# Attention, routed experts and a second layer on one core: first-expert weights loaded later and rounded on GpSimd, v crossed one step later, sums work moved out of the first expert, all rests on VectorE

## The chip, the cores and the metric

The kernel runs on one core of a Trainium2 chip. The metric is device time in microseconds (us), lower is better. In the tables PE is TensorE (PEld its weight loads), DVE is VectorE, ACT is ScalarE, POOL is GpSimd and SP is the engine that here only issues transfers. An engine takes its instructions in the order in which they stand in its queue, so an instruction that waits holds all behind it.

## The reference, cut to what matters

```python
# q, k, v: (8, 8, 576, 64); tokens N = 4608, model width 512
scores = scale * np.matmul(q_c, k_c.transpose(0, 1, 2, 4, 3))   # chunks of 64 tokens
attn = softmax(scores); x = np.matmul(attn, v_c)                # -> x: (4608, 512)
do_compute = x @ w_skip > 0
e_idx = np.argmax(x[do_compute] @ w_gate, axis=1)               # 8 experts, one per token
for e in range(8):
    h = np.maximum(xc[mask] @ w1[e], 0.0)                       # 512 -> 1024
    y[mask] = gate_w[mask, None] * (h @ w2[e])                  # 1024 -> 512
x[do_compute] = xc + y
h = np.maximum(np.maximum(x @ w1, x @ w2), x @ w3)              # 512 -> 768, all tokens
return h @ w_out
```

## The kernel before, in words

**Attention and routing.** The 4608 tokens are 36 tiles of 128. A loop of 36 steps does one tile per step, and each stage of a tile runs one step behind the stage before it. In step t TensorE multiplies the exponentials of tile t-2 with v (`xp`), makes the scores of tile t (`sc`), turns exponentials (`trp`), q and k of the next pair of tiles (`trq`, `trk`), makes gate logits of tile t-3 (`lp`) and turns x of tile t-2 (`trx`). ScalarE empties the turned tiles (`aT`, `qT`, `kT`, `xt`, `lg`) and takes the exponentials (`ex`). VectorE does row maxima, scaling and routing. GpSimd rearranges q and k (`qr`, `kr`), scatters token numbers (`ids_dram`) and stores x in groups of four tiles (`x_dram`). Half of each v tile must also lie on the other 64 partitions: `cross` copies one half on GpSimd and `cross_up` the other on ScalarE (`vm`); v has eight buffers, and the load of v of tile t+6 is asked for in step t. SP issues the loads of q, k, v and of weights in one queue; the q and k of the last two pairs of tiles come as 16 small transfers each.

**Weights.** Matmuls run in three passes on a rounded part and its rest: `whi` is the weight rounded to fp32r, `wlo` is the raw weight minus `whi`. An expert has eight pieces of 128x1024. Those of the first expert (`raw_e_0` to `raw_e_7`) are loaded and split amid the attention loop: load at step c-5, `whi` on ScalarE at step c, `wlo` a step later on VectorE (two of them on GpSimd), for c in `CUTS` (12, 16, 18, 20, 24, 26, 28, 32). `raw` tiles have three buffers.

**Behind the loop.** Tokens are routed in groups of four tiles, the last four in two groups of two. The first two tiles of expert 0 use tokens known early; its third tile waits for the last groups (`ids_0`, found by a matmul). In the tail TensorE's order is written by hand, and the products of expert 0 (`h`) are placed by `behind` between pieces of routing; the order on the other engines is left to the scheduler after step 33. Then come the third and fourth tile of expert 0, and experts 1 to 7 in the same way, each with the split of the next expert's weights beside it (pieces 1, 3 and 7 take their rests on GpSimd). `sums_ahead` prepares weights of the second layer in chunks: `STEPS` says how many ride with each expert (2, 2, 2, 2, 2, 1, 0, 0).

**The second layer** runs over all tokens from about 500 us on; the change does not touch it.

Of the kernel before, what the change touches and what calls it, by code (L numbers as in the profile page):

```python
# [40 lines left out]
def kernel(  # L41
# [102 lines left out]
    SIZES = [GT] * (NT // GT - 1) + [2, 2]  # L144
# [165 lines left out]
    def scaled(t):  # L310
        xp = units[t // 2]["xp", t % 2]
        g, j = PLACE[t]
        if j == 0:
            if g == len(SIZES) - 1:
                parts = [four_kb([P, 1, XW], F32, f"xg{g}_{i}", True) for i in range(SIZES[g])]
            else:
                parts = [bpool.tile([P, GT, XW], F32, tag="xg", name=f"xg{g}")[:, :SIZES[g], :]]
# [117 lines left out]
    def place(g):  # L435
# [20 lines left out]
        if START[g] >= DIRECT:  # L456
            place_first(g, oh, lo, hi)

    def place_first(g, oh, lo, hi):
        t0, nt = START[g], SIZES[g]  # L460
        found = ps_sm(f"ids_0_ps{g}")[:, :1]
        lo_f = apool.tile([P, 2], F32, tag="lo_f", name=f"lo_f{g}", bufs=1)
        nc.vector.tensor_copy(lo_f, lo[:, :nt])
        hi_f = apool.tile([P, 2], F32, tag="hi_f", name=f"hi_f{g}", bufs=1)
        nc.vector.tensor_copy(hi_f, hi[:, :nt])
        tok = apool.tile([P, 2], F32, tag="tok0", name=f"tok0_{g}", bufs=1)
        nc.vector.tensor_tensor(tok, oh[:, :nt, 0], tok_f[:, t0:t0 + nt], op=ALU.mult)
        for j in range(nt):
            row = apool.tile([P, P], F32, tag="row", name=f"row{t0 + j}")
            nc.vector.tensor_scalar(row, col_f, lo_f[:, j:j + 1], None, op0=ALU.is_equal)  # L470
            val = apool.tile([P, 1], F32, tag="val", name=f"val{t0 + j}")
            link["val"] = nc.vector.tensor_scalar(
                val, col_f[:, 2:3], hi_f[:, j:j + 1], tok[:, j:j + 1], op0=ALU.is_equal, op1=ALU.mult)
            link["found", g] = nc.tensor.matmul(found, row, val, start=j == 0, stop=j == nt - 1)
        nc.vector.tensor_tensor(ids_0[:, 2:], ids_0[:, 2:], found, op=ALU.add)
# [138 lines left out]

    for u in range(5):
# [11 lines left out]
    LAG, late, raws_0 = GT + 5, range(NT - 2), {}  # L627
    HAND = NT - 2
    CUTS = [12, 16, 18, 20, 24, 26, 28, 32]
    ASIDE = (18, 26)  # L630
    routing = {}
    fetch = None
    in_order = ExitStack()
    in_order.enter_context(tc.manual_schedule(engines={mybir.EngineType.PE}))
    by_hand = ExitStack()
    by_hand.enter_context(tc.manual_schedule(
        engines={getattr(mybir.EngineType, n) for n in ("DVE", "Activation", "Pool")}))

    def last_of(t):
        if 0 <= t < NT:  # L640
            g, j = PLACE[t]
            if j + 1 == SIZES[g]:
                return g
        return None

    for t in range(NT + LAG):
        u, s = divmod(t, 2)
        hand = t < HAND
        if t == HAND:
            by_hand.close()  # L650
        ranked = last_of(t - 5) if hand else None
        if ranked is not None:
            rank_out(ranked)
        if hand and t - LAG in late:
# [12 lines left out]
        if 0 <= t - 2 < NT:  # L667
            values(t - 2)
            scaled(t - 2)
        if t >= 2 and t - 2 + NV < NT:  # L670
            load_v(t - 2 + NV)
        if t + 5 in CUTS:
            i = CUTS.index(t + 5)
            with tc.issue_after(link["load"].ins):
                raws_0[i] = load_raw(*expert_src(0, i))
        if t < NT:
            scores(t)
            shift(t)
        if 0 <= t - 1 < NT:
# [3 lines left out]
        if 0 <= t - 3 < NT:  # L683
# [4 lines left out]
        if t < NT:  # L688
            exponentials(t)
        g = last_of(t - 3)  # L690
        if g is not None and hand:
            route(g)
        if 0 <= t - 2 < NT:
            x_transpose(t - 2)
            x_out(t - 2)
        if t < NT:
            cross_up(t)
        if g is not None and not hand:
            route(g)
            gates(g)  # L700
        g = last_of(t - 4)
        if g is not None:
            if t <= HAND:
                gates(g)
            rank_of(g)
            if not t + 1 < HAND:
                rank_out(g)
        g = ranked if hand else last_of(t - 4)
        if g is not None:
# [3 lines left out]
            if g == FIRST or START[g] + SIZES[g] == DIRECT:  # L713
                for i in range(max(late[0], t - LAG + hand), START[g + 1]):
                    send_id(i)
                late = range(START[g + 1], NT - 2)
            if START[g] + SIZES[g] == DIRECT:
                load_ids(ids_0[:, 2:], ids_rows[:, 2:3])
            if g == FIRST:
# [5 lines left out]
        if t in CUTS:  # L725
            i = CUTS.index(t)
            hi_0 = wpool.tile([P, 1024], F32R, tag="w", name=f"whi_e0_{i}")
            lo_0 = wpool.tile([P, 1024], F32R, tag="w", name=f"wlo_e0_{i}")
            nc.scalar.copy(hi_0, raws_0[i])
            ew[0, i] = hi_0, lo_0  # L730
        if t - 1 in CUTS:
            i = CUTS.index(t - 1)
            hi_0, lo_0 = ew[0, i]
            (nc.gpsimd if t - 1 in ASIDE else nc.vector).tensor_tensor(lo_0, raws_0[i], hi_0.bitcast(F32), op=ALU.subtract)
            ew[0, i] = [w.rearrange("p (a b) -> p a b", a=2) if i > 3 else w for w in ew[0, i]]
# [5 lines left out]
        if not hand and t - LAG in late:  # L741
            send_id(t - LAG)
    in_order.close()
# [12 lines left out]
    first_accs = []  # L756

    def first_acc(name):
        if not first_accs:
            two = two_banks("xp" if turns["half"] else "sc", name)  # L760
            turns["half"] = True
            first_accs.extend([two[:, 0], two[:, 1]])
        return first_accs.pop(0)

    turns["half"] = False
# [22 lines left out]
    def mm3(acc, ahi, alo, bhi, blo, first, last, onto=False):  # L788
        nc.tensor.matmul(acc, ahi, bhi, start=first, stop=False, skip_group_check=onto)  # L789
        nc.tensor.matmul(acc, ahi, blo, start=False, stop=False, skip_group_check=onto)  # L790
        return nc.tensor.matmul(acc, alo, bhi, start=False, stop=last, skip_group_check=onto)  # L791

# [5 lines left out]

    KF_ORDER = [6, 7, 4, 5, 0, 1, 2, 3]

    def second(name, key, hhi, hlo, i, xg, ids, tag=None):
# [3 lines left out]
        for n, kf in enumerate(KF_ORDER):  # L805
            bhi, blo = ew[key[0], 4 + kf // 2]
            with tc.issue_after(link["found", 9].ins) if tag and n > 2 else nullcontext():
                mm3(acc, hhi[:, kf, sl], hlo[:, kf, sl], bhi[:, kf % 2, :], blo[:, kf % 2, :], n == 0, n == 7)
        put_back(key, xg, ids, acc)

    def first_tiles(name, e, xT, xgs, idss, between, side=(), behind=None):
# [5 lines left out]
        for n in range(0, 8, per):  # L817
            f0 = KF_ORDER[n]
            acc = (first_acc if e == 0 else ps_mm)(f"h_{name}_{n}")[:, :per * w].rearrange("p (f t) -> p f t", f=per)
            for j in range(per):  # L820
                f = f0 + j
                with tc.issue_after(behind[n + j].ins) if behind else nullcontext():
                    for c in range(KC):
                        ahi, alo = ew[e, c]
                        link["h"] = mm3(acc[:, j, :], ahi[:, f * P:(f + 1) * P], alo[:, f * P:(f + 1) * P],
                            hi[:, c, :], lo[:, c, :], c == 0, c == KC - 1)
# [5 lines left out]
        for i in range(2):  # L832
            second(f"{name}_{i}", (e, i), hhi, hlo, i, xgs[i], idss[i], "tr" if e == 0 else None)
# [30 lines left out]
    STEPS = [2, 2, 2, 2, 2, 1, 0, 0]  # L864
# [124 lines left out]
    xT[0] = rows_T("0", xgs[0])  # L989
# [3 lines left out]
    for t in range(NT - 2, NT):  # L993
# [17 lines left out]
    for e in range(E):  # L1011
# [23 lines left out]
        if e + 1 < E:  # L1035
            with ExitStack() as pinned:
                if e == 0:
                    for k in ("val", "routed"):
# [5 lines left out]
        behind = [link[k] for k in (  # L1044
            ("x", NT - 1), ("logits", NT - 1), ("rank", 8), ("logits", NT - 1), ("found", 8), ("rank", 9),
            ("found", 9), ("found", 9))] if e == 0 else None
        h_e = first_tiles(
            f"{e}", e, xT[e], xgs[e], [idc(e, 0), idc(e, 1)], ahead, side, behind)
        raws = {i: load_raw(*expert_src(e + 1, i)) for i in LATE} if e + 1 < E else {}
        if e == 0:  # L1050
            turn_ahead()
            with tc.issue_after(link["rows"][0].ins), tc.issue_after(link["rows"][1].ins):
                for chunk in later:
                    chunk()
# [5 lines left out]
        with ExitStack() as pinned:  # L1060
            if e == 0:
                single("0_2", (0, 2), *third, turn_next)
                for ins in link["rows"]:
                    pinned.enter_context(tc.issue_after(ins.ins))
            elif e + 1 < E:
# [168 lines left out]
```

## Time and profile before

| what | value |
|---|---|
| median of 3 runs (lowest, highest) | 1087.12 us (1084.63, 1091.06) |
| the profiled execution | 1093.87 us, of it 1092.1 us from first to last instruction |
| TensorE busy in it | 1015.1 us, 93% |
| VectorE, ScalarE, GpSimd busy | 570.8, 431.2, 359.6 us |
| mean granted TensorE clock | 0.961 |

TensorE is busy nearly all the time, so the question for each stretch is why it stood there and at which clock it ran. The stretches used below are the loop until its first long stall (9.63 to 59.81 us), the loop with stalls (to 155.37), its last steps (to 176.17), the tail until the third tile of expert 0 begins (to 218.40), and the rest of expert 0 (to 269.68).

### The profile page before, as it was taken

To read this page: it belongs to the slowest core of one execution; us is meant where nothing else is said; L and a number is where in the kernel's file an instruction comes from. 1 tells how busy PE (TensorE), PEld (TensorE's weight loads), DVE (VectorE), ACT (ScalarE), POOL (GpSimd) and SP (SyncE) were. 2 spreads that over 40 slices of the span, in tenths; PEclk is the share of its full clock that TensorE was granted. 3 is DMA by queue.
4 is the path that set the end of the run, shared out by engine and by line. 5 is a ranking of instruction groups with operands and counts; after the bars stand their busy time and mean duration, and the time that the engine had idled before them with its cause. 6 is when DMAs were issued, how large, how long until landed. Compare 5 with 4: busy or idle time off the path is not lost.

```text
span 1092.1 us, 19781 instructions
## 1 busy us (share of the span) xinstructions
PE 1015.1 (93%) x7570; PEld 867.2 (79%) x7570; DVE 570.8 (52%) x1100; ACT 431.2 (39%) x771; POOL 359.6 (33%) x381
## 2 busy tenths in 40 slices
PE   8978878979999979997998999999999999999996
PEld 7977768958878868885876788888877888888995
DVE  5766756569737376433688833335144443444241
ACT  5867755335425244322444342223222232223231
POOL 4557555545513263311333140123122140124011
PEclk9989978989999989998999899999999999999998
DMA  9999684467738185428998545663566546666581
GB/s 238 266 293 284 182 198 162 139 222 255 285 111 285 56 300 196 164 83 255 289 325 285 174 158 160 200 186 120 164 183 184 151 136 192 191 201 197 190 254 39
DMA packets 212050, 217.14 MB, mean 199 GB/s; under 512 B 47195, under 2 KB 176235, under 8 KB 211936
## 3 DMA queue, kind: packets, MB, share of 16 engines
q1 hardware_dynamic: 198688, 174.16, 54.1%
q0 software_dynamic: 10656, 33.22, 8.6%
q10 hardware_dynamic: 2592, 8.26, 2.0%
q8 instruction: 70, 1.15, 0.4%
q14 instruction: 44, 0.36, 0.1%
HBM read 175.15 MB, written 41.83 MB: 199 GB/s over the span
## 4 chain that ended last, share of the span: by engine, by line
PE 46%; DMA 5%; issue 1%; DVE 1%; POOL 1%; ACT 0%; SPq 0%; POOLq 0%; DVEq 0%; ACTq 0%
PE f_a L789 6%; PE f_a L791 6%; PE f_a L790 6%; PE o L789 5%; PE o L791 4%; PE o L790 4%; PE f_d L789 3%; PE f_d L790 3%; PE f_d L791 3%; DMA ws<-m_sums 3%; PE f_b L789 1%; PE f_b L791 1%; PE f_b L790 1%; DMA m_sums<-n_q 1%; PE trf L963 1%
## 5 line engine op out<-in xcount | busy, mean ns | idle before, releaser
L94 POOL TENSOR_TENSOR fh<-best,fh 128x512 fp32r<-128x512 f32 (+1 forms) x60 | 75.0, 1255 | 356.6 <-ACT fh L93 271.5
L789 PE MATMUL f_a<-x_t,ws 128*128 128x512 f32 (+1 forms) x270 | 100.4, 373 | 2.7 <-ACT u L1128 2.7
L791 PE MATMUL f_a<-x_t,ws 128*128 128x512 f32 (+1 forms) x270 | 100.1, 371 | 0.0
L790 PE MATMUL f_a<-x_t,ws 128*128 128x512 f32 (+1 forms) x270 | 100.0, 371 | 0.0
L789 PE MATMUL h<-xhi,whi_e 128*128 128x256 f32 x256 | 75.3, 295 | 13.5 <-ACTq L1066 7.2
L790 PE MATMUL o<-wlo_m,fh 128*128 128x512 f32 x216 | 84.6, 391 | 0.0
L93 ACT CAST whi_e<-raw_e 128x1024 fp32r<-128x1024 f32 x56 | 57.7, 1050 | 67.0 <-DMA raw_e<-in_moe_w_dram 35.6
L789 PE MATMUL o<-whi_m,fh 128*128 128x512 f32 x216 | 83.9, 392 | 0.0
L791 PE MATMUL o<-whi_m,fh 128*128 128x512 f32 x216 | 83.3, 393 | 0.0
L789 PE MATMUL y<-whi_e,hhi 128*128 128x512 f32 x184 | 74.1, 404 | 0.6 <-ACT hhi L856 0.6
L790 PE MATMUL h<-xlo,whi_e 128*128 128x256 f32 x256 | 74.6, 292 | 0.1
L791 PE MATMUL h<-xhi,wlo_e 128*128 128x256 f32 x256 | 74.1, 291 | 0.0
L791 PE MATMUL y<-whi_e,hlo 128*128 128x512 f32 x184 | 73.2, 401 | 0.2
L790 PE MATMUL y<-wlo_e,hhi 128*128 128x512 f32 x184 | 72.5, 396 | 0.0
L94 POOL TENSOR_TENSOR wlo_e<-raw_e,whi_e 128x1024 fp32r<-128x1024 f32 x21 | 53.0, 2531 | 57.0 <-ACT whi_e L93 55.7
L93 ACT CAST fh<-best 128x512 fp32r<-128x512 f32 (+1 forms) x60 | 34.6, 579 | 89.8 <-DVE best L1119 60.8
L789 PEld LDWEIGHTS h<-xhi,whi_e 128*128 128x128 f32 x256 | 51.1, 199 | 16.3 <-ACTq L1066 10.2
L789 PEld LDWEIGHTS f_a<-x_t,ws 128*128 128x128 f32 x270 | 51.2, 190 | 12.0 <-ACT u L1128 3.5
L1122 ACT COPY p<-f_a 128x512 f32<-128x512 f32 (+1 forms) x45 | 24.4, 545 | 90.8 <-PE f_a L791 90.6
L791 PEld LDWEIGHTS f_a<-x_t,ws 128*128 128x128 f32 x270 | 51.3, 190 | 8.7
L780 POOL DMA_INDIRECT x_dram<-xg,ids_sb x20 | 20.8, 1041 | 112.9 <-DVEq L1004 46.8
L790 PEld LDWEIGHTS f_a<-x_t,ws 128*128 128x128 f32 x270 | 51.2, 190 | 8.5
(230 smaller groups left out, 2699.5 us busy)
## 6 DMA issues: line engine op xcount, KB each, us to landing
ws<-m_sums SPq DMA_DIRECT2D x135, 512.0 KB
raw_e<-in_moe_w_dram SPq DMA_DIRECT2D x64, 512.0 KB
ws<-m_sums SPq DMA_DIRECT2D x45, 256.0 KB
x<-x_dram SPq DMA_DIRECT2D x36, 256.0 KB
x_dram<-xg POOLq DMA_DIRECT2D x8, 1040.0 KB, 7.7
v_all<-in_v_dram SPq DMA_DIRECT2D x32, 256.0 KB
out_dram<-os SPq DMA_DIRECT2D x32, 256.0 KB
m_sums<-n_raw ACTq DMA_DIRECT2D x18, 448.0 KB
```

The costliest lines, as they stand in the source:

```text
L93: nc.scalar.copy(hi, src),
L94: eng.tensor_tensor(lo, src, hi.bitcast(F32), op=ALU.subtract),
L780: ins = nc.gpsimd.indirect_dma_start(out=x_dram[:, :], out_offset=bass.IndirectOffsetOnAxis(ap=ids, axis=0), in_=xg, in_offset=None, bound ...
L789: nc.tensor.matmul(acc, ahi, bhi, start=first, stop=False, skip_group_check=onto)
L790: nc.tensor.matmul(acc, ahi, blo, start=False, stop=False, skip_group_check=onto)
L791: return nc.tensor.matmul(acc, alo, bhi, start=False, stop=last, skip_group_check=onto)
L963: nc.tensor.transpose(tr[:, i * P:(i + 1) * P], row[:, c * P:(c + 1) * P], ident)
L1122: nc.scalar.copy(p1, acc_a)
```

## The change

First, the loads of the first expert's weights are asked for at steps 15 to 27 (before: 7 to 27), five of the eight into buffers of their own; GpSimd rounds seven of them and ScalarE one; VectorE makes all rests. `ROUND` lists piece, step of the load, engine and step of the rounding, step of the rest. Second, `cross(t - 1)` and `cross_up(t - 1)` run in step t, the second between `kT` and `ex`. Third, the last four tiles are one group, and the tail of the loop is written out by hand for four engines, with the first products of expert 0 in eight parts. Fourth, expert 0 gets no chunk of `sums_ahead` (`STEPS`). Fifth, VectorE makes the rests of all experts' weights.

```diff
-    SIZES = [GT] * (NT // GT - 1) + [2, 2]
+    SIZES = [GT] * (NT // GT)
...
+    def head_part(n):
+        hi, lo = HEAD["xT"]
+        if n % 2 == 0:
+            HEAD["acc", n // 2] = first_acc(f"h_0_{n}").rearrange("p (f t) -> p f t", f=2)
+        f = KF_ORDER[n]
+        for c in range(KC):
+            ahi, alo = ew[0, c]
+            link["h"] = mm3(HEAD["acc", n // 2][:, n % 2, :], ahi[:, f * P:(f + 1) * P], alo[:, f * P:(f + 1) * P],
+                hi[:, c, :], lo[:, c, :], c == 0, c == KC - 1)
...
-    CUTS = [12, 16, 18, 20, 24, 26, 28, 32]
-    ASIDE = (18, 26)
+    ROUND = [
+        (0, 15, "Pool", 19, 21),
+        (1, 18, "Pool", 23, 25),
...
+        (4, 26, "Pool", 35, 37),
+        (5, 27, "Act", 36, 37),
+    ]
...
+    def rounded(t):
+        for i, _, eng, at, _ in ROUND:
+            if at == t:
+                ew[0, i] = [wpool.tile([P, 1024], F32R, tag="w", name=f"w{nm}_e0_{i}") for nm in ("hi", "lo")]
+                (nc.gpsimd.tensor_copy if eng == "Pool" else nc.scalar.copy)(ew[0, i][0], raws_0[i])
...
-        if t < NT:
-            cross(t)
+        if t >= 1:
+            cross(t - 1)
...
-        if t < NT:
-            exponentials(t)
+        if t >= 1:
+            cross_up(t - 1)
+        exponentials(t)
...
-        if t < NT:
-            cross_up(t)
...
-            (nc.gpsimd if t - 1 in ASIDE else nc.vector).tensor_tensor(lo_0, raws_0[i], hi_0.bitcast(F32), op=ALU.subtract)
...
+    head_start(xT[0])
+    head_part(0)
+    x_transpose(NT - 1)
+    x_out(NT - 1)
+    rests(36)
+    head_part(1)
+    logits(NT - 1)
+    logits_out(NT - 1)
+    head_part(2)
+    route(LAST_G)
+    gates(LAST_G)
+    rank_of(LAST_G)
+    rank_out(LAST_G)
+    head_part(3)
...
-    STEPS = [2, 2, 2, 2, 2, 1, 0, 0]
+    STEPS = [0, 2, 2, 2, 2, 2, 1, 0]
...
-                    expert_piece(e + 1, i, free.pop(0), nc.gpsimd if i % 2 else None)
+                    expert_piece(e + 1, i, free.pop(0))
```

Where the instructions stand, at three places. The first is SP's queue. `v_all_130` to `v_all_137` are the eight v buffers in turn, so `v_all_135` is here v of tile 13, and `raw_e_0` is piece 0. Before, from the load of v of tile 12 on:

```order
L216 DMA v_all_134<-in_v_dram 128x8x64
L210 DMA qkt_881<-in_q_dram 128x8x128
L210 DMA qkt_881<-in_k_dram 128x8x128
L216 DMA v_all_135<-in_v_dram 128x8x64
L100 DMA raw_e_0_806<-in_moe_w_dram 128x1024
L216 DMA v_all_136<-in_v_dram 128x8x64
L210 DMA qt_1072<-in_q_dram 128x8x128
L210 DMA kt_1073<-in_k_dram 128x8x128
```

And now, one round of the buffers later, from v of tile 21 on:

```order
L216 DMA v_all_135<-in_v_dram 128x8x64
L701 DMA raw_e_0_230<-in_moe_w_dram 128x1024
L216 DMA v_all_136<-in_v_dram 128x8x64
L216 DMA v_all_137<-in_v_dram 128x8x64
L210 DMA qt_2100<-in_q_dram 128x8x128
L210 DMA kt_2101<-in_k_dram 128x8x128
L216 DMA v_all_130<-in_v_dram 128x8x64
L701 DMA raw_e_1_231<-in_moe_w_dram 128x1024
```

Piece 0 stood right behind v of tile 13 and now stands right behind v of tile 21, behind five more pairs of q and k; ahead of v of tile 28 there stood six pieces (0 to 5), and now three (0 to 2).

The second place is GpSimd's queue at step 19, where before no weight stood; now, from the crossing of tile 18 to that of tile 19:

```order
L223 COPY vm_1993<-v_all_132 64x260
L235 COPY qr_1_1995<-qt_1286 128x512
L235 COPY kr_1_1997<-kt_1287 128x512
L502 DMA x_dram<-xg_1501 128x4x520
L709 CAST whi_e_0_2092<-raw_e_0_230 128x1024
L480 DMA ids_dram<-tok_i,rslot_1790 36864x1
L223 COPY vm_2104<-v_all_133 64x260
```

The rounding of piece 0 stands between the store of x and the crossing of tile 19.

The third place is ScalarE's queue at the third tile of expert 0 (`h_2_1s` and `h_2_0s` are the two halves of its product). Before:

```order
L538 CAST xhi_2_4245<-trm_2_0_4247 128x512
L555 ACTIVATE n_q_4256<-n_raw_4254 128x512
L555 ACTIVATE n_q_4272<-n_raw_4270 128x512
L849 ACTIVATE h_2_1s<-h_2_1_4526 128x512
L596 CAST n_raw_4254<-n_q_4256 128x896
L596 CAST n_raw_4270<-n_q_4272 128x896
L598 DMA m_sums_0_149<-n_raw_4254 128x896
L598 DMA m_sums_0_149<-n_raw_4270 128x896
L849 ACTIVATE h_2_0s<-h_2_0_4541 128x512
```

And now:

```order
L539 CAST xhi_2_4186<-trm_2_0_4188 128x512
L929 ACTIVATE h_2_1s<-h_2_1_4435 128x512
L929 ACTIVATE h_2_0s<-h_2_0_4450 128x512
L539 CAST xhi_4479<-trm_0_4481 128x4x128
L936 CAST hhi_2_4433<-trh_2_1_4465 128x512
L936 CAST hhi_2_4433<-trh_2_0_4472 128x512
```

The instructions of two chunks that stood between the two halves are gone from here.

## Rows read from the trace of the kernel before

**Rows 1.** Stretches: length, busy by engine, granted clock, DMA share, GB/s
```profile
9.63:59.81 50.18, 48.55 (x1088) 45.02 (x1091) 37.89 (x107) 39.69 (x83) 25.94 (x49) 1.00 1.09 261
59.81:155.37 95.56, 74.03 (x1531) 67.78 (x1526) 59.57 (x176) 63.74 (x132) 56.36 (x80) 0.87 0.91 241
155.37:176.17 20.80, 20.05 (x447) 18.57 (x445) 16.09 (x47) 16.35 (x36) 12.16 (x22) 0.94 0.84 214
176.17:218.40 42.23, 39.66 (x334) 36.07 (x325) 22.61 (x101) 13.87 (x27) 21.50 (x22) 0.84 0.37 128
218.40:269.68 51.28, 40.94 (x225) 34.69 (x224) 41.88 (x57) 22.20 (x32) 23.74 (x15) 0.90 0.70 237
```
**Rows 2.** Waits of TensorE, 0 to 260 us: total, times, longest
```profile
PE trx L337 <- ACT aT L292: 20.6, 5, 7.0
PE trh L854 <- ACT h_0s L849: 7.3, 1, 7.3
```
**Rows 3.** Waits of ScalarE and GpSimd, 0 to 200 us
```profile
ACT whi_e L729 <- DMA raw_e<-in_moe_w_dram: 14.3, 4, 5.7
...
ACT vm L229 <- DMA v_all<-in_v_dram: 6.4, 3, 5.3
...
POOL vm L223 <- DMA v_all<-in_v_dram: 24.3, 7, 9.7
```
**Rows 4.** Stretches: q and k whole, then in small transfers
```profile
40.00:106.70 66.70, 56.80 (x1246) 52.63 (x1244) 46.80 (x141) 49.44 (x103) 45.16 (x71) 0.95 1.09 287
106.70:144.60 37.90, 33.22 (x700) 30.67 (x701) 26.46 (x84) 27.68 (x59) 21.17 (x29) 0.86 0.64 188
```
**Rows 5.** Timeline of SP: start, length, what; v of tiles 13, 28
```profile
56.59 1.67 SPq L216 DMA_DIRECT2D v_all<-in_v_dram  x1
58.31 2.60 SPq L100 DMA_DIRECT2D raw_e<-in_moe_w_dram  x1
...
144.58 2.16 SPq L216 DMA_DIRECT2D v_all<-in_v_dram  x2
```
**Rows 6.** Timeline of ScalarE, step 12; in brackets idle before
```profile
66.88 1.04 ACT L729 CAST whi_e<-raw_e 128x1024 fp32r<-128x1024 f32 x1 [5.73 <-DMA raw_e<-in_moe_w_dram]
```
**Rows 7.** Timeline at steps 29 and 30, all engines
```profile
149.65 0.41 ACT L229 COPY vm<-v_all 64x260 f32<-64x260 f32 x1 [5.25 <-DMA v_all<-in_v_dram]
...
149.70 0.39 POOL L223 COPY vm<-v_all 64x260 f32<-64x260 f32 x1 [9.66 <-DMA v_all<-in_v_dram]
...
151.82 1.04 ACT L729 CAST whi_e<-raw_e 128x1024 fp32r<-128x1024 f32 x1 [1.76 <-DMA raw_e<-in_moe_w_dram]
...
154.45 0.37 PE L305 MATMUL xp<-v_all,aT 64*64 64x65 f32 x1
```
**Rows 8.** Stretches behind the loop at half the clock
```profile
181.80:195.50 13.70, 13.63 (x124) 12.67 (x120) 7.60 (x41) 3.77 (x9) 5.90 (x7) 0.50 0.23 79
229.60:239.90 10.30, 5.99 (x18) 4.73 (x19) 6.36 (x14) 4.51 (x7) 1.03 (x1) 0.50 0.88 319
```
**Rows 9.** Timeline at the third tile of expert 0
```profile
222.13 6.23 DVE L554 SCALAR_TENSOR_TENSOR n_q<-n_raw,n_q 128x512 int32<-128x512 int32 x2
...
223.11 4.70 POOL L94 TENSOR_TENSOR wlo_e<-raw_e,whi_e 128x1024 fp32r<-128x1024 f32 x2
...
231.08 1.78 ACT L596 CAST n_raw<-n_q 128x896 fp32r<-128x896 f32 x2 [7.47 <-DVE n_q L593]
...
233.91 1.12 PE L854 MATMUL trh<-ident,h_0s 128*128 128x128 f32 x4 [7.34 <-ACT h_0s L849]
```
**Rows 10.** Groups: busy us, mean ns | idle; the third of the whole span
```profile
L235 POOL COPY qr<-qt 128x512 f32<-128x512 f32 x20 | 12.3, 614 | 13.1 <-DMA qt<-in_q_dram 12.1
...
L734 DVE TENSOR_TENSOR wlo_e<-raw_e,whi_e 128x1024 fp32r<-128x1024 f32 x6 | 7.3, 1220 | 15.3 <-ACT whi_e L729 15.3
...
L94 POOL TENSOR_TENSOR wlo_e<-raw_e,whi_e 128x1024 fp32r<-128x1024 f32 x21 | 53.0, 2531 | 57.0 <-ACT whi_e L93 55.7
```
**Rows 11.** Timeline of TensorE where a later expert begins
```profile
403.22 0.58 PE L789 MATMUL h<-xhi,whi_e 128*128 128x256 f32 x1 [7.16 <-ACTq L1066]
```

More of the change, by code (lines that the diff above doesn't have):

```diff
@@ L313, in scaled @@
         if j == 0:
[L314 to L317, printed above, removed]
+            parts = [bpool.tile([P, GT, XW], F32, tag="xg", name=f"xg{g}")]
             groups[g] = parts, apool.tile([P, GT, E + 1], F32, tag="lg", name=f"lg{g}")
@@ L639, in last_of, with weights_ahead @@
     def last_of(t):
[L640 to L646, printed above, removed]
+        return PLACE[t][0] if 0 <= t < NT and PLACE[t][1] == GT - 1 else None
+    def weights_ahead(t):
+        for i, at, *_ in ROUND:
+            if at == t:
+                src, name, shape = expert_src(0, i)
+                with tc.issue_after(link["load"].ins):
+                    if i in (0, 1, 2, 3, 7):
+                        a = shape[0]
+                        nc.sync.dma_start(raws_0[i].rearrange("p (a b) -> p a b", a=a) if a > 1 else raws_0[i], src)
+                    else:
+                        raws_0[i] = load_raw(src, name, shape)
@@ L647 @@
+    for t in range(NT):
         u, s = divmod(t, 2)
[L648 to L651, printed above, removed]
+        ranked = last_of(t - 5)
         if ranked is not None:
             rank_out(ranked)
-        if hand and t - LAG in late:
+        if t - LAG in late:
             send_id(t - LAG)
@@ L666 @@
             nc.gpsimd.tensor_copy(col_f, col_i)
[L667 removed]
+        if t >= 2:
             values(t - 2)
             scaled(t - 2)
[L670 to L675, printed above, removed]
[L676 to L679 removed]
+            if t - 2 + NV < NT:
+                load_v(t - 2 + NV)
+        weights_ahead(t)
+        scores(t)
+        shift(t)
+        if t >= 1:
             exp_transpose(t - 1)
@@ L724 @@
                 fetch = t + 3
[L725 to L733, printed above, removed]
-            (nc.gpsimd if t - 1 in ASIDE else nc.vector).tensor_tensor(lo_0, raws_0[i], hi_0.bitcast(F32), op=ALU.subtract)
-            ew[0, i] = [w.rearrange("p (a b) -> p a b", a=2) if i > 3 else w for w in ew[0, i]]
+        rounded(t)
+        rests(t)
         if t == fetch:
@@ L740 @@
                 gather(xgs[0][j], at[:, j:j + 1], rows)
-        if not hand and t - LAG in late:
-            send_id(t - LAG)
-    in_order.close()
+    LAST_G = len(SIZES) - 1
+    rank_out(LAST_G - 1)
+    cross(NT - 1)
+    cross_up(NT - 1)
+    for t in range(NT - LAG, DIRECT - 4):
+        send_id(t)
+    values(NT - 2)
+    scaled(NT - 2)
+    logits(NT - 3)
+    logits_out(NT - 3)
+    xT[0] = rows_T("0", xgs[0])
+    exp_transpose(NT - 1)
+    x_transpose(NT - 2)
+    x_out(NT - 2)
+    place(LAST_G - 1)
+    for t in range(DIRECT - 4, DIRECT):
+        send_id(t)
+    load_ids(ids_0[:, 2:], ids_rows[:, 2:3])
+    values(NT - 1)
+    scaled(NT - 1)
+    logits(NT - 2)
+    logits_out(NT - 2)
+    rounded(36)
+    head_start(xT[0])
[12 more added lines that the diff above has]
+    head_part(3)
+    head_relu(0)
+    head_relu(1)
+    place(LAST_G)
+    place_first(LAST_G)
+    head_part(4)
+    head_part(5)
+    found_first(LAST_G)
+    head_rest(0)
+    rests(37)
+    head_rest(1)
+    head_part(6)
+    head_part(7)
+    head_relu(2)
+    head_relu(3)
+    head_rest(2)
+    head_rest(3)
+    by_hand.close()
     cp = ps_sm("cnt_ps")[:, :E]
@@ L992 @@
     gather(xgs[0][2], idc(0, 2))
-    for t in range(NT - 2, NT):
+    for t in range(DIRECT, NT):
         send_id(t)
@@ L1064 @@
                     pinned.enter_context(tc.issue_after(ins.ins))
+                for chunk in later:
+                    chunk()
             elif e + 1 < E:
```

146 lines of the change are left out of this document (80 added, 66 removed).

## The prediction

> **What bounds the kernel now.** I read the stretches first [rows 1]. TensorE is the engine that sets the end: in the quiet part of the loop it is busy 48.55 of 50.18 us, 13 steps at 3.86 us each. The next 17 steps take 95.56 us where 17 x 3.86 would be 65.6, so the stretch loses 30 us. The tail (42.23 us) and the rest of expert 0 (51.28 us) lose too: both run in part at the lower clock, and the second has 10 us without TensorE work. The waits of TensorE name what it stood for [rows 2]: 20.6 us in five waits for ScalarE's `aT`, one of 7.3 us for `h_0s`. But `aT` is only next in ScalarE's queue. ScalarE itself [rows 3] waits 14.3 us for raw weights of expert 0 and 6.4 us for v, and GpSimd 24.3 us for v. So the loop is bound by arrivals, through queues that stand in order. Two states of the transfers follow each other [rows 4]: until 106.7 us the DMA share is 1.09 at 287 GB/s, which is full; then, with q and k in small pieces, 0.64 at 188 GB/s, where SP's issuing one by one is the limit.
>
> **The loop: later weights and later crossing.** The decisive arrival is v of tile 28. SP issues it at 144.58 [rows 5], it lands at 149.65, where both ScalarE and GpSimd stood for it [rows 7], and TensorE multiplies with it at 154.45. SP's order decides when it can leave: six weight pieces stand ahead of it before, three now. A piece is 128 x 1024 x 4 bytes = 0.52 MB, 1.8 us at 287 GB/s, and 2.60 us as SP's issue of piece 0 shows [rows 5]. Three fewer are 5.5 to 7.8 us; I take 6, so v lands at 143.7. Before, 4.8 us passed from landing to the product: the crossing, 1.76 us of waiting for another raw piece, its rounding of 1.04 us, then `aT` [rows 7]. Now ScalarE crosses (0.41), and nothing but that stands between: 0.8 us, so the product starts at 144.5 instead of 154.45. That is 10 us. The last steps, 20.80 us, I leave as they are, since their clock and rate are nearly the full ones. Bounds: 0 if the small transfers, which are the same 32, hold v just as long as before; above, the bytes of the stretch, 95.56 x 241 = 23.0 MB less three pieces, 21.4 MB, at 287 GB/s are 75 us, so 21.
>
> The rounding on GpSimd has no row. Nearest are its copy of 128x512 in 614 ns, which doubled is 1.2 us, and its two-input pass over 128x1024 in 2531 [rows 10]; I take 1.3, and GpSimd has time (56.36 busy of 95.56 [rows 1]). Worse is what the rounding waits for. Piece 0 now leaves after v of tile 21: behind the 56.59 of tile 13 [rows 5] come five pairs of q and k (5 x 1.05 MB), eight tiles of v (8 x 0.26) and two stores of x (2 x 1.06), 9.5 MB or 33 us at 287 GB/s, so at 89.7; with the 8.6 us from 58.31 to 66.88 that it took before [rows 5, 6] it lands at 98.3. GpSimd reaches it at the end of step 19, 59.81 + 7 x 3.86 = 86.8. So there is a new wait of 11 us, behind which stand the scatter, the crossing of tile 19 and the next q and k, and TensorE waits for that crossing at step 21 for some 10 us, until about 101. I cost this at nothing: eight more steps bring step 29 to 132, and v of tile 28 is still on the way until 143.7. That is the cover, 11 us; if v came sooner, this wait would be the price.
>
> **The tail.** TensorE is busy 39.66 of 42.23 us [rows 1], but 13.63 of that ran at 0.50 of the clock, the level of 1.2 GHz [rows 8]; the same work at 2.4 GHz is 6.8 us shorter. All of it is still to be done: 32.8 us. Now parts of the first products stand between each link of the routing chain, and the row maxima of the last tile come ahead of the gates of the group before. I take 34.7, a gain of 7.5. Bounds: 9.4 if no idle time stays; a loss of 3 if the thin start still ends in the low clock and VectorE's four rests (4 x 1.22 us [rows 10]) delay routing by 3 of their 4.9.
>
> **The third tile of expert 0.** VectorE worked on sums for two chunks, ScalarE's rounding of them waited 7.47 us, behind it stood `h_0s`, and TensorE waited 7.34 [rows 9]. TensorE then ran at 0.50, 5.99 us busy [rows 8], which costs 3.0. Both chunks leave expert 0: up to 10.3. I take 9.5, since `h_0s` still follows a product that ends shortly before. Bounds 6 and 10.3.
>
> **Later experts.** 21 rests move from GpSimd (2531 ns) to VectorE (1220) [rows 10]: 26 us more on VectorE, which is free for more than that beside TensorE, and raw buffers come free about 1.3 us sooner each. TensorE stood 7.16 us at one start of an expert behind ScalarE's late rounding [rows 11]. I take 1 gained; bounds a loss of 6 (VectorE late with a rest of the hidden layer at six experts, 1 each) and a gain of 6. Here a rule speaks for more. Beside two of GpSimd's rests (4.70 us) two passes of VectorE took 6.23 [rows 9]. The Trainium skill (SBUF — State Buffer, Who interferes with whom) has it that an instruction of VectorE with two inputs in SBUF and one of GpSimd that reads SBUF block each other whole; by that rule VectorE is freed of these blocks, the 7.16 us go altogether, and the sum below is 34 instead of 28. The trace agrees for that pair, but no row ties the 7.16 to it, so I stay with 1.
>
> **Sum.** 10 + 7.5 + 9.5 + 1 = 28 us off the profiled execution of 1093.87 (span 1092.1 and 1.8 around it): 1065.9. That execution is 6.75 above the median of the runs, 1087.12; against the median it is 1059.
>
> **Rivals.**
> A. The loads set the loop's end and it does not move. For it: SP issues the same 32 small transfers, and 37.90 us of the loop pass at share 0.64 [rows 4]. Against it: pieces leave from ahead of v, and the full part before them is shortened by their bytes. Gain 18, time 1069. The Trainium skill (DMA: Bandwidth & Descriptors, Issuing engines are not separate DMA queues) says that transfers of all engines end on the same 16 engines; by it the moved bytes only return later, which is this rival; the share of 0.64 says that there is room for them, so the trace bears it out little.
> B. The chunks stall as much at experts 5 and 6, where they go: 10.3 back, time 1069. For it: VectorE carries the rests as well there. Against: experts 1 to 4 carry two chunks each and show no wait like rows 9.
> C. The stalls all go, v included: loop gain 21, time 1048. For it: the bytes allow it; against it: the small transfers.
> D. Slower. GpSimd's four roundings at steps 31, 32, 34 and 35 wait for pieces that leave behind v of tiles 29 to 32. There no later arrival covers them; each full wait, 11 us as at step 19, holds a crossing and with it TensorE for some 10. Three of them eat the 28 us, so from three on it is slower; four give 40 less 28, 1099. For it: the queue is in order, and piece 3 would leave at about 141. Against: with 8.6 us it lands at 150, and step 31 ends at about 152.
>
> **How the numbers follow.** The forecast, 1059, has 0.48, with 1051 to 1068 as its own range; A 0.15, B 0.09, C 0.14, D 0.07; 0.07 is left for two terms failing at once with the tail's low clock staying, some 1084. The range from 1043 to 1080 takes in A, B and C and the bounds of the terms, and leaves out D and the last. 0.5% (5.4 us) is about what a measurement can tell here. Faster 0.86, within it 0.07, slower 0.07.
>
> **What would show it.** Right: ScalarE has no waits for raw weights in the loop; GpSimd one of about 11 us at piece 0 near 87 to 98; v of tile 28 is crossed near 144, and the last scores begin near 166; from there to the third tile some 35 us without a long half-clock stretch; no wait of 7 us for `h_0s`. Wrong: v of tile 28 at 149 (A), the long wait at piece 0 repeated at pieces 3, 7, 6 and 4 (D), or waits for `n_raw` at experts 5 and 6 (B). I am wrong altogether if TensorE's waits shrink and the time does not.

## The result and the profile after

The changed kernel takes 1075.55 us (median of 4 runs, 1070.48 to 1079.05) against 1088.59 for the kernel before beside it: ratio 0.9868 [0.9832, 0.9903], 13 us faster where I had forecast 28. Later runs on other chips gave 0.9875 and 0.9899. (One later profile, of the second run with all edits, was taken in a slower execution and is not read.) The direction held, the tail came near its size and the third tile within its bounds; the loop gained nothing.

The stretches of the changed kernel, cut at the same places as [rows 1] (same columns; first scores, step 13, step 30, last scores, first transposes for the third tile, expert 1):

```profile
9.16:69.31 60.15, 52.68 (x1084) 47.59 (x1087) 38.12 (x108) 40.30 (x83) 27.10 (x50) 0.94 1.12 270
69.31:151.29 81.98, 73.32 (x1534) 67.21 (x1530) 57.53 (x173) 59.19 (x125) 52.93 (x81) 0.98 0.87 233
151.29:178.07 26.78, 23.08 (x450) 21.33 (x446) 16.96 (x51) 15.38 (x33) 15.52 (x23) 0.87 0.70 150
178.07:213.60 35.53, 34.61 (x337) 31.68 (x330) 24.29 (x79) 14.63 (x28) 16.35 (x17) 0.95 0.54 182
213.60:258.71 45.11, 39.95 (x225) 33.74 (x224) 30.16 (x45) 19.62 (x28) 15.61 (x13) 0.96 0.64 214
```

Line by line against [rows 1]: the first 13 steps are 10.0 us longer, the next 17 are 13.6 shorter, the last 5 are 6.0 longer; so the loop loses 2.4 where I forecast 10 gained. The tail gains 6.7, the third tile 6.2. From there to the last product of the experts it is 239.2 us against 240.8, and the rest 579.4 against 581.6; with 0.5 at the start the sum is the 14.8 by which the spans differ (1092.1 and 1077.3).

The waits of TensorE (total, times, longest) in the first 260 us, which answer to [rows 2]:

```profile
PE xp L305 <- ACT vm L229: 12.4, 29, 0.5
PE sc L264 <- issue: 4.7, 3, 2.3
PE h L617 <- DVEq L1146: 2.2, 1, 2.2
```

The long waits for `aT` and `h_0s` are gone. In their place stands a short one, 29 times: in nearly every step TensorE waits for ScalarE's copy of v's half. ScalarE's own waits for raw weights and v [rows 3] no longer appear in the loop. One quiet step, from ScalarE's timeline (start, length, in brackets the idle time before):

```profile
116.40 0.63 ACT L251 COPY kT<-trk 128x512 f32<-128x512 f32 x1 [0.32 <-PE trk L249]
117.05 0.41 ACT L229 COPY vm<-v_all 64x260 f32<-64x260 f32 x1
117.48 0.63 ACT L282 ACTIVATE ex<-ex 128x512 f32<-128x512 f32 x1
```

and from TensorE's in the same step:

```profile
116.20 0.60 PE L334 MATMUL trx<-ident,xg 128*128 128x128 f32 x4
116.73 0.33 PE L305 MATMUL xp<-v_all,aT 64*64 64x65 f32 x2
117.51 0.27 PE L305 MATMUL xp<-vm,aT 64*64 64x65 f32 x2 [0.46 <-ACT vm L229]
```

TensorE is at `xp` at 117.05, and the copy that it multiplies with begins only then, since it stands behind `kT`. `ex` is later by the copy as well. The cycle closes: the products, the scores, the transposes of the exponentials and of k come behind one another on TensorE, then `kT`, then the copy, then the next products. A quiet step takes 4.60 us instead of 3.84; over 36 steps that is 27 us, about what the arrivals had cost.

A second place appears at the loop's end. VectorE waits for the first expert's row numbers, by its timeline in this execution:

```profile
163.87 0.17 DVE L785 TENSOR_SCALAR at<-ids 128x2 int32<-128x2 int32 x1 [2.39 <-DMA ids<-ids_dram]
```

and in a later execution of the same kernel:

```profile
166.25 0.17 DVE L785 TENSOR_SCALAR at<-ids 128x2 int32<-128x2 int32 x1 [8.97 <-DMA ids<-ids_dram]
```

Of [rows 10], from the groups: GpSimd's rounding, which had no row before, took 1043 ns, and none of the seven waited (0.1 us idle in sum); the rests of later experts are VectorE's now.

```profile
L709 POOL CAST whi_e<-raw_e 128x1024 fp32r<-128x1024 f32 x7 | 7.3, 1043 | 0.1
...
L94 DVE TENSOR_TENSOR wlo_e<-raw_e,whi_e 128x1024 fp32r<-128x1024 f32 x56 | 67.5, 1221 | 15.1 <-ACT whi_e L93 12.3 <-ACTq L1146 2.0 <-DVEq L1079 0.7
```

Of [rows 8], the only half-clock stretch of the tail, by the stretches view:

```profile
183.70:187.10 3.40, 3.40 (x31) 2.97 (x33) 2.04 (x7) 2.08 (x5) 1.66 (x3) 0.50 0.75 285
```

And of [rows 9], ScalarE's timeline at the third tile: `h_0s` follows its product, with nothing before it in the queue:

```profile
224.27 0.60 ACT L929 ACTIVATE h_0s<-h 128x512 f32<-128x512 f32 x1 [2.13 <-PE h L619]
```

### The profile page after: what moved, and what is told of

Its sections match the earlier page's. It is cut to its first block, busy times and chain, and to the rows that moved or that the text cites. A ratio compares the mean times of both kernels' runs of the same rounds, so it can differ in the third digit from the quotient of the medians.

```text
span 1077.3 us, 19677 instructions
## 1 busy us (share of the span) xinstructions
PE 1012.0 (94%) x7569; PEld 864.2 (80%) x7569; DVE 570.1 (53%) x1098; ACT 427.2 (40%) x763; POOL 316.0 (29%) x361
## 4 chain that ended last, share of the span: by engine, by line
PE 43%; DMA 5%; issue 3%; DVE 2%; POOL 1%; SPq 0%; ACT 0%; POOLq 0%; DVEq 0%; ACTq 0%
PE f_a L617 5%; PE f_a L618 5%; PE f_a L619 5%; PE o L617 5%; PE o L619 5%; PE o L618 5%; PE f_d L617 3%; PE f_d L619 3%; PE f_d L618 3%; DMA ws<-m_sums 2%; DMA m_sums<-n_q 2%; PE f_b L617 1%; PE f_b L618 1%; PE f_b L619 1%; PE trf L1043 1%
## 5 line engine op out<-in xcount | busy, mean ns | idle before, releaser
L869 POOL DMA_INDIRECT x_dram<-xg,ids_sb x20 | 27.1, 1356 | 201.8 <-DVE xg L867 94.3
L94 DVE TENSOR_TENSOR wlo_e<-raw_e,whi_e 128x1024 fp32r<-128x1024 f32 x56 | 67.5, 1221 | 15.1 <-ACT whi_e L93 12.3
```

Of the source, the lines that this page charges most:

```text
L94: eng.tensor_tensor(lo, src, hi.bitcast(F32), op=ALU.subtract),
L869: ins = nc.gpsimd.indirect_dma_start(out=x_dram[:, :], out_offset=bass.IndirectOffsetOnAxis(ap=ids, axis=0), in_=xg, in_offset=None, bound ...
```

## The experiments

The time of the kernel before differs between chips (1089 to 1098 us), so only ratios to it, and runs on one chip, are compared; the four chips of the experiments are called A to D. A ratio too moves from chip to chip: that of the changed kernel from 0.9868 to 0.9899. "Loop" is from the first scores to the last ones: 166.5 us before; 168.9, 171.2 (chip B) and 175.4 (chip D) in three profiled executions of the changed kernel.

**The copy's place.** Four kernels on chip A; the first has the copy behind qT.

```diff
             qk_transpose(u + 1, s, "q")
+        if t >= 1:
+            cross_up(t - 1)
...
-        if t >= 1:
-            cross_up(t - 1)
         exponentials(t)
```

> The changed kernel, with one call moved: ScalarE copies v's upper half of tile t-1 behind qT in step t, no longer behind kT. Theory (place): in the changed kernel each step of the loop takes 4.60 us because the copy ends 0.46 us after TensorE is free for the products of that tile, and TensorE's next work hangs on it; moved 1.1 us ahead, the copy is done before TensorE asks, the quiet steps fall to 3.85 to 3.95 us, the 0.46 us waits for vm go, and the loop is then held by v of tile 28 as I forecast (landing near 144, last scores near 166 where they are at 178 now): 1063 to 1066 us. Rival (arrivals): the loads set the loop's end; steps get quicker in between but v or weights are waited for, last scores near 176 to 178, time 1073 to 1076. Rival (queue): it is not the place but one more copy in ScalarE's full step; the steps stay at 4.4 to 4.6, time 1073 to 1076.

Measured: 0.9839 [0.9796, 0.9882], loop 170.2. The quiet steps fell to 3.84 us and the 29 waits went: the place explains the 4.60 us. But the end of the loop did not move, as the rival on arrivals had it (last scores at 179.4). The time came back in two waits, and some 38 us of the loop ran at the granted clock of 0.5 (17 in the changed kernel). TensorE's two longest waits in this run:

```profile
PE lp L345 <- DVE sm L319: 8.2, 1, 8.2
PE xp L305 <- POOL vm L223: 7.3, 1, 7.3
```

GpSimd's timeline at the second of them:

```profile
100.96 1.04 POOL L709 CAST whi_e<-raw_e 128x1024 fp32r<-128x1024 f32 x1 [7.38 <-DMA raw_e<-in_moe_w_dram]
```

and VectorE's at the first:

```profile
165.97 0.17 DVE L785 TENSOR_SCALAR at<-ids 128x2 int32<-128x2 int32 x1 [9.68 <-DMA ids<-ids_dram]
```

GpSimd's is the wait for piece 0 that I had forecast at 11 us (landing at 98.3; it was 101). VectorE's is the one I had not seen: it waits at `at` for the row numbers, and TensorE's wait is listed under `sm`, which only stands behind. SP issued that load at 159.26, after pieces 6, 4 and 5, as its timeline shows:

```profile
145.94 2.38 SPq L100 DMA_DIRECT2D raw_e<-in_moe_w_dram  x1
...
150.32 1.40 SPq L100 DMA_DIRECT2D raw_e<-in_moe_w_dram  x1
...
154.36 1.08 SPq L100 DMA_DIRECT2D raw_e<-in_moe_w_dram  x1
...
159.26 1.12 SPq L496 DMA_DIRECT2D ids<-ids_dram  x1
```

**The whole crossing as before.** `cross(t)` at the start of step t and `cross_up(t)` behind `x_out(t - 2)`, and the two calls after the loop removed.

> The changed kernel, with both halves of v's crossing put back where the kernel before has them: GpSimd's for tile t at the start of step t, ScalarE's for tile t at the end of step t. Theory (place): quiet steps 3.85 us; the copy is done a whole step before its products, but ScalarE stands in its queue for a v that is needed only two steps later, so the loop ends some 4 us behind the run with the copy behind qT (v of tile 28 is waited for in step 28, not 29): last scores near 169, 1066 to 1070 us. Rival (arrivals): last scores near 176, 1074. If the later weights were worth nothing, the waits for v in ScalarE and GpSimd come back at 20 to 30 us in sum as before.

Measured: 0.982 [0.9769, 0.9871], loop 169.7, quiet steps 3.84 us. GpSimd and ScalarE stood 11 us each for v of tile 28, and TensorE 9.4 us for `aT` behind them, the picture of [rows 7]. The last scores came at 179.0, where the theory had 169. The two runs with quick steps are not told apart (0.9839 and 0.982), so no run shows that crossing a step later is worth anything; what is shown is that its place behind `kT` costs 0.76 us a step.

**The kernel before with the crossing of the change.**

```diff
-        if t < NT:
-            cross(t)
+        if 1 <= t <= NT:
+            cross(t - 1)
...
+        if 1 <= t <= NT:
+            cross_up(t - 1)
         if t < NT:
             exponentials(t)
...
-        if t < NT:
-            cross_up(t)
```

> The kernel before, with the crossing alone changed: GpSimd copies v of tile t-1 at the start of step t, ScalarE copies its half of tile t-1 in step t between kT and the exponentials. Theory (place): every quiet step goes from 3.84 to 4.60 us with a wait for vm of 0.46 us; the waits for v and raw weights shrink by what the steps grow, since SP's order is unchanged and v of tile 28 still lands near 149, so the loop's end moves by 0 to 6 us and the time is 1087 to 1095. Rival (the 4.60 us come from the later weights or from rounding on GpSimd): steps stay at 3.84 to 3.95, and the crossing that comes a step later takes waiting for v away: 1080 to 1087.

Measured: 1.0042 [1.0014, 1.007], quiet steps 4.60 us, loop 176.8, and TensorE's costliest wait in the loop is the short one again:

```profile
PE xp L305 <- ACT vm L229: 13.2, 29, 1.4
```

The crossing alone makes the kernel before slower by some 5 us; the rival that put the 4.60 us on the weights is out.

**Row numbers ahead of pieces.** Chip B, with the changed kernel beside (0.9875 [0.9844, 0.9907]). The three pieces are put behind the row numbers in SP's queue.

```diff
-        (6, 25, "Pool", 34, 36),
-        (4, 26, "Pool", 35, 37),
-        (5, 27, "Act", 36, 37),
+        (6, 29, "Pool", 34, 36),
+        (4, 30, "Pool", 35, 37),
+        (5, 31, "Act", 36, 37),
```

With the copy behind qT:

> The run with the copy behind qT, and the three last pieces of expert 0 (6, 4, 5) put into SP's queue at steps 29, 30, 31, behind the load of the first expert's row numbers, not at 25, 26, 27 ahead of it. Theory (arrivals behind the last v): with the copy behind qT the loop still ended at 179.4 since VectorE stood 9.7 us for those row numbers at step 32, behind pieces in SP's queue; now they land some 8 us sooner, that wait and the half clock after it go, last scores at 166 to 170, some 10 us faster than with the copy alone (ratio to the kernel before 0.974 to 0.978). Rival (bytes): the bytes only change places; the pieces come late for their rounding at steps 34 to 36, TensorE waits there or in the tail, and the time is that of the copy alone (ratio 0.982 to 0.986).

With the copy left where the change has it:

> The changed kernel with only the three pieces later in SP's queue (steps 29, 30, 31), the copy of v left behind kT. Theory: the steps stay at 4.60 us, which cover most of the wait for the row numbers; the 2.4 us wait of VectorE at step 31 and the 4 us that it costs go, so 2 to 4 us faster than the changed kernel, far from what both edits give together. Rival (the row numbers are the cause and the copy's place is nothing): 8 us or more faster.

And with the copy behind qT and `(0, 15, "Pool", 21, 23)`:

> The copy behind qT and the three pieces later, and piece 0 rounded by GpSimd in step 21 and finished by VectorE in step 23, two steps later than it was. Theory: the wait of GpSimd at step 19, 7.4 us, for which TensorE stood 7.3, goes, but v of tile 28 still is not there before 144 to 146, so that TensorE waits that much longer at step 29: within 3 us of the run without this edit, less what the half clock behind the wait cost. Rival (v follows the steps): SP's queue moves up with the steps, and it is 5 to 8 us faster.

> The changed kernel once more, beside the others of this call on one chip: ratio to the kernel before 0.983 to 0.990 as first measured. It is the base for the three others.

Measured: 0.9809 [0.9783, 0.9834] with a loop of 164.0; 0.9772 [0.9747, 0.9798] with 168.1; 0.9819 [0.978, 0.9857] with 162.9. The waits of VectorE for the row numbers fell from 8.97 us (the changed kernel on this chip) to 1.0, none and 0.4. The later pieces alone are 9 us faster than the changed kernel (1068.08 against 1077.03), as the rival of that run had it: taking the pieces from ahead of the row numbers was worth more here than the copy's place. I had sized it by the 2.4 us of one execution; the second showed 9.0, and the third, on chip D, no wait at all, since VectorE came to `at` only at 170.16. That the 9 us went by way of this wait is argued and not shown: the two profiled executions of this chip do not have the gain (spans 1072.7 with the later pieces and 1070.7 without, the loop 3.1 us shorter). With the copy moved as well the loop is shorter, but the times are no better, and the intervals overlap. In the first of these two runs the tail gave the loop's gain back: it took 40.6 us, 13.7 of them at half the clock, against 34.8; for the second why is open. What was then late is v of tile 28, by TensorE's waits in the third run:

```profile
PE xp L305 <- DMA v_all<-in_v_dram: 7.1, 1, 7.1
```

and by SP's timeline there:

```profile
104.80 3.65 SPq L204 DMA_DIRECT2D qt<-in_q_dram  x4
...
140.65 0.63 SPq L204 DMA_DIRECT2D kt<-in_k_dram  x1
141.39 3.27 SPq L216 DMA_DIRECT2D v_all<-in_v_dram  x2
```

SP issues the 32 small loads of q and k, with three loads of v and one piece among them, from 104.80 to 141.28, and v of tile 28 stands behind the last. This is the cover of 11 us in my forecast, and the mechanism of my rival A.

**Half as many loads.** One load for each sequence with all heads takes the place of one for each head. The first run has all edits: this one, the copy behind qT, the later pieces and piece 0 rounded later.

```diff
-            for h in range(H):
+            for b in range(nb):
+                pr = slice(b * TAIL // 2, (b + 1) * TAIL // 2)
                 for dst, src in ((qt, q), (kt, k)):
                     link["load"] = nc.sync.dma_start(
-                        dst[:, h, :], src[b0:b0 + nb, h, WHOLE:, :].rearrange("b (p r) d -> b p (r d)", r=2))
+                        dst[pr], src[b0 + b, :, WHOLE:, :].rearrange("h (p r) d -> p h (r d)", r=2))
```

> The run with the copy behind qT, the three pieces later and piece 0 rounded later, and with q and k of the last two units loaded in 16 transfers (one for each sequence, all heads) in place of 32 (one for each head, four sequences). The bytes and their grain are the same. Theory (SP's issuing): SP issues the 32 one behind the other from 104.8 to 141.4, and v of tile 28 leaves at 141.4 since it stands behind them; with half as many it leaves some 10 us sooner, the 7.1 us for which TensorE stood for it go and with them the half clock behind; the loop takes some 153 to 157 us where it took 162.9, ratio 0.970 to 0.976. Rival (the transfers' rows, not their number): SP's issues take twice as long each or the rows land no sooner, v of tile 28 lands at 147 as before, ratio as without the edit.

> The changed kernel with the three pieces later and 16 transfers in place of 32, and the copy of v left behind kT. Theory: the steps of 4.60 us set the end by now, no v is waited for, so an earlier v is worth nothing: the loop stays at 166 to 168 us and the time within 2 us of the run with the later pieces alone (ratio 0.975 to 0.980). Rival (SP's issuing sets the end here too): 5 us or more faster.

Measured, chip C: 0.975 [0.9712, 0.9789] (1060.08 us) with a loop of 150.3 in one execution; with the copy left behind `kT` 0.9834 [0.9788, 0.9879] (1069.01 us) with a loop of 164.4, a little shorter than expected, at a ratio above the expected one. With all edits v of tile 28 leaves at 123.42 instead of 141.39, by SP's timeline:

```profile
122.96 0.31 SPq L205 DMA_DIRECT2D kt<-in_k_dram  x1
123.42 3.75 SPq L217 DMA_DIRECT2D v_all<-in_v_dram  x2
```

and TensorE no longer waits for it. Where steps of 4.60 us set the pace, the same edit leaves a loop 14 us longer. That is the clearest reading of the copy's price: once v and the row numbers are not late, its place (with piece 0's rounding, which differs too) is worth 14 us of loop and 0.8% of the time.

Chip D, with the changed kernel beside (0.9899 [0.9865, 0.9933]): all edits again, and all edits without the later pieces.

> All edits once more, beside the changed kernel on one chip: some 14 us faster than it (ratio to the kernel before 0.971 to 0.977), the loop 150 to 153 us.

> The run with all edits, but pieces 6, 4 and 5 back at steps 25, 26, 27, ahead of the row numbers of the first expert in SP's queue. Theory (three in a row): the loop is held by whichever comes last of v, row numbers and ScalarE's copy; here VectorE waits for the row numbers again, some 5 to 10 us, and the loop takes 156 to 162 us where all edits gave 150. Rival (the row numbers were late only since the small transfers pushed everything back): with 16 transfers they land in time, loop 150 to 152.

Measured: 0.9685 [0.9644, 0.9725], where the same edits gave 0.975 on chip C, and 0.9681 [0.965, 0.9712]. Without the later pieces VectorE waits 4.6 us for the row numbers and the loop takes 156.8 us, as the theory had it, but the time is the same: with 16 loads the edit of the pieces adds nothing that can be measured. Both are some 20 us faster than the changed kernel on that chip (1066.76 and 1064.84 against 1086.11), where I had expected some 14 of all edits, and the best versions here.

**Chunks and rests.** On chip A, the chunks alone put back (`STEPS = [2, 2, 2, 2, 2, 1, 0, 0]`, issued behind the gathered rows as before):

> The changed kernel, with the sums' chunks back at the experts of the kernel before (two in expert 0, none in expert 6) and at that place in the code. Theory: the wait of TensorE for h_0s and the half-clock stretch come back at the third tile, 5 to 10 us slower than the changed kernel (1081 to 1086). Rival: the chunks cost as much wherever they stand, since the same VectorE and GpSimd work waits at experts 5 and 6: within 2 us of the changed kernel (1074 to 1078).

Measured: 0.9912 [0.9874, 0.9949], 0.1 to 0.4% above the changed kernel's ratios on other chips, which is about what one kernel's ratio moves between chips; from the third tile to expert 1 46.9 us (45.1, 44.2 and 45.5 in the changed kernel), and no wait for `h_0s`. That is nearer to the rival: the 7.34 us of [rows 9] are not the chunks' alone. On chip C the rests of the odd pieces went back to GpSimd, alone and with the chunks:

```diff
-                    expert_piece(e + 1, i, free.pop(0))
+                    expert_piece(e + 1, i, free.pop(0), nc.gpsimd if i % 2 else None)
```

> The changed kernel, with the rests of the odd pieces of later experts' weights on GpSimd again, the chunks of the sums left where the change has them. Theory (GpSimd's two-input passes slow VectorE's beside them): passes of VectorE that lie beside a rest of GpSimd take 2.5 to 3 us where 0.7 is usual, the start of an expert waits some us as in the kernel before; 3 to 8 us slower than the changed kernel (ratio 0.990 to 0.995 where that has 0.987). Rival (my forecast's 1 us): within 2 us of it.

> The changed kernel with both the chunks and the rests of the odd pieces back as before. Theory: it was the rests on GpSimd, not the chunks alone, that held the third tile: with both back two passes of VectorE take some 6 us, the wait of TensorE for h_0s of some 5 to 7 us returns, which the run with only the chunks back did not show, and the stretch from the last transposes of the first tile's rows to expert 1 goes from 46.9 to about 50 us. Ratio 0.992 to 1.000. Rival (chunks alone; the first products in the tail have made the third tile free of it): no such wait, 46 to 47 us.

Measured: 0.9992 [0.9962, 1.0023] and 1.0009 [0.998, 1.0037]. With the rests alone there is no wait for `h_0s`, and the stretch takes 44.1 us. With both back the wait is there again and the stretch takes 52.6. TensorE's longest wait there:

```profile
PE trh L934 <- ACT h_0s L929: 6.0, 1, 6.0
```

VectorE's timeline ahead of it:

```profile
224.88 0.29 DVE L592 TENSOR_TENSOR n_q<-n_q 128x128 f32<-128x128 f32 x1
225.08 3.13 DVE L591 TENSOR_TENSOR n_q<-n_q 128x128 f32<-128x128 f32 x1
228.14 0.28 DVE L592 TENSOR_TENSOR n_q<-n_q 128x128 f32<-128x128 f32 x1
```

and GpSimd's:

```profile
225.66 2.40 POOL L94 TENSOR_TENSOR wlo_e<-raw_e,whi_e 128x1024 fp32r<-128x1024 f32 x1
```

A pass of VectorE that takes 0.29 us took 3.13: begun 0.58 us before GpSimd's rest, it ended 0.15 us behind it. Two later passes did the same: together 3.32 us from 228.74 on, where 0.48 is usual, beside a rest of 2.37 us. With the chunks back but the rests on VectorE the same chain of passes ran at its usual length: the pass that took 6.23 us for two in [rows 9] took 1.28 there. So the wait needed both, the chunks in that place and GpSimd's rests beside them; neither alone brought it. The Trainium skill (SBUF — State Buffer, Who interferes with whom) says that VectorE's second port pair is GpSimd's own and that the lock on it excludes the other; the trace agrees, 3.13 us beside 2.40. Why the pass that by this profile began first is the one that was held stays open.

The same two runs answer rival B. Moving the chunks away with the rests on GpSimd takes 8.6 us from the third tile (52.6 to 44.1) and puts 6.6 on the later experts (235.8 to 242.4, one execution each), and the times are the same. So with the rests on GpSimd the chunks cost nearly as much where they went.

The rests alone had stood on another chip than the changed kernel, so on chip D they are repeated beside it.

> The changed kernel, the base of this call: ratio 0.983 to 0.992.

> The changed kernel with the rests of the odd pieces of later experts on GpSimd again, beside the changed kernel on one chip. Theory (GpSimd's passes slow VectorE's): 6 to 12 us slower than the changed kernel, so that the rests are most of what the change gained. Rival (my forecast): within 2 us of it, and the difference seen was the chip's.

Measured: 0.9899 [0.9865, 0.9933] with the rests on VectorE, 1.0012 [0.9985, 1.0039] with the odd ones on GpSimd: 1.1%, or 12 us. In the profiles the part from expert 1 to the last product of the experts is 11.0 us longer (234.8 and 245.8), and what is behind it 3.8. Single executions place such a loss only roughly: the changed kernel alone has 239.2, 235.3 and 234.8 for that part. TensorE's longest waits at the starts of experts, with the odd rests on GpSimd:

```profile
PE h L617 <- ACTq L1146: 11.7, 2, 7.5
```

and with all on VectorE:

```profile
PE h L617 <- PEq L1146: 5.8, 2, 3.5
```

The wait of 7.16 us [rows 11] is one of this kind: it stands 133.5 us behind the start of expert 1; at the same start of an expert TensorE waits 7.46 us with the odd rests on GpSimd and 1.39 with all on VectorE. And the sign that I had named for rival B, ScalarE waiting for VectorE ahead of its rounding into `n_raw`, shows late in the experts with the odd rests on GpSimd (9.2 us in three waits from 400 us to 515) and not with all on VectorE (0.3 us in one).

## Why the prediction was wrong

**The loop (10 us) is the term that failed**, and with it nearly the whole of the miss: 28 less 14.8 is 13.2, and the loop alone came 12.4 short. (The third tile's 3.3 and the tail's 0.8 short are made up by 0.6 in the experts, and by 2.2 behind them and 0.5 at the start, for which the forecast had no term.) I wrote of the new crossing "nothing but that stands between: 0.8 us", and multiplied the quiet steps by 3.86 as before. I followed the copy for the one tile whose v was late, and not for the other 35. In the new order the copy ends a step's chain (`trk`, `kT`, copy, `xp`), and each step costs 4.60 us. The kernel before with this crossing shows it alone (1.0042), and so do the steps of 3.84 us once the copy is behind qT.

**"The last steps, 20.80 us, I leave as they are"** failed too: 26.8 here. By estimate 3.8 of the 6.0 us more are the 0.76 us of five steps; the rest is about the wait for the row numbers (2.4). I did not follow the load of the row numbers through SP's queue, where three pieces now stood just ahead of it; the wait was 2.4 and 9.0 us in two executions and nothing in a third, and putting the pieces behind it was worth 9 us on one chip.

**v of tile 28** did leave earlier, at 137.7 in place of 144.58 [rows 5], 6.9 us where I had 6; nobody waited for it, as the steps were late by then. With the copy behind qT and the pieces later it was the limit again. Rival A, which left the loop's gain at 0 and had 0.15, came nearest in the time of the loop, by another mechanism in the changed kernel; its own mechanism showed when the others were out of the way.

**The roundings on GpSimd**: 1.3 us forecast, 1.04 measured. The wait at piece 0 came only where steps were quick (7.4 us for 11). Rival D did not come. Rival C, a loop gain of 21 us, is what all edits together came near: 150.3 us, 16 less than before.

**The tail**: 7.5 forecast, 6.7 measured. The half-clock stretch of 13.7 us [rows 8] is one of 3.4 here. The kernel before with the new crossing keeps 42.0 us, 13.7 of them at half clock; no run takes the tail's edit back alone. In the first two runs with the copy behind qT 13.7 us at half clock came back and the tail took 40.4 and 40.6 us; the other variants of the changed kernel have 34.8 to 37.8. So part of the gain can be lost. Both runs had stalled late in the loop, but so had the changed kernel on chip B (9.0 us, tail 34.8), so what brings the low clock back is open.

**The third tile**: 9.5 forecast, 6.2 measured, and for a reason half wrong. I gave it to the chunks; the runs give it to the chunks with GpSimd's rests (46.9 us with the chunks alone back, 44.1 with the rests alone, 52.6 with both).

**Later experts**: 1 forecast. The single comparison of stretches shows 1.6, but beside the changed kernel on one chip the rests are worth 12 us. The two do not count the same: the 12 us are against a kernel that has the chunks in the later experts already, and there the rests on GpSimd go with a longer expert part (242.4 and 245.8 us) than with the chunks where they were before (235.8 us, and 240.8 in the kernel before; one execution each). I had priced the rests here and the moved chunks as rival B, each for itself; the runs speak for the one deciding the price of the other. This is the term that I sized most wrongly, though it was not the one that made me miss: the row (6.23 us beside 4.70) was there, the rule beside it in the prediction spoke for a gain, and I stayed with 1 since no row tied the 7.16 to it. Why the first execution's expert part shows so little of it (239.2, against 235.3 and 234.8 in two others) stays open; TensorE stood longer in it (15.1 us against 13.0 and 13.6) and was busy longer (224.2 against 222.3 and 221.2), at a granted clock of 0.98 against 0.99.

## What to carry to other kernels

When a step of a pipelined loop is moved, walk it for the quiet step first: what it stands behind on its engine, who asks for it, and whether that closes a cycle; a move that cures one late arrival is paid in all the others. Take out waits one after the other, and expect the next: here copy, row numbers and small loads each hid behind another, and the loop went from 169 us to 150 with all three dealt with. Two edits that share an engine are priced together: here the moved chunks cost the later experts little only with the rests off GpSimd. Small loads that one engine issues in a row are a queue like any other; ask what stands behind the last.

## What was not expected of the hardware

A 128x1024 rounding pass with one input took GpSimd 1043 ns, where its pass with two inputs takes 2531 [rows 10]. A load of a quarter of the partitions for all heads, with twice the bytes, cost SP no more than one of all partitions for one head (0.71 us on average over the 16, 0.94 over the 32), so that half the loads let v of tile 28 leave some 18 us sooner with the same bytes.
